# Attention units taken in pairs, and a tile's rows turned behind a pair's turns

## The chip, the cores and the metric

One Trainium2 chip (trn2), one core. The metric is the device time of the whole kernel in microseconds: the median of three runs, beside one profiled execution with its trace.

## The reference

Three stages follow on each other, all in float32 at the interface.

- Attention: batch 4, 8 heads, 576 positions, head size 64. Scores are q·kᵀ/8; a score lower than its row's maximum less tau is dropped; softmax over what is left; product with v.
- A mixture of experts over the 2304 tokens of width 512: noisy logits (x·w_gate plus log(1 + exp(x·w_noise)) times noise), the two highest of 8 experts, softmax of the two; each expert is relu(x·w1)·w2 with 1024 hidden channels.
- A dense layer pair with 2048 hidden channels and a leaky relu with a slope per channel, giving the output of 2304 × 512.

## The kernel before, in words

The whole program is written out by hand, one instruction after another, and each engine works through its own instructions in the order in which they are emitted. The change lies in the attention stage, up to about 300 us.

**Units.** The 80 entries of `units` (lines 323 to 329) are the attention's steps. A whole unit is one batch, one block of 128 queries and one pair of heads; four units (the four pairs of heads) make up one tile of 128 tokens, 18 tiles in all. The last 64 queries of a batch make tail units ("t", one score block for both heads): units 16 to 23 and 56 to 63.

**The pieces of a unit**, each a small function (lines 333 to 438):

- `s_mm` (L347): the scores on TensorE, 12 matmuls (6 for a tail unit) from q and k split into high and low parts, into one PSUM tile `ps_s` for each head. There are two of these tiles.
- `d1` (L358): VectorE scales and negates the scores into `m_tmp` and takes their minimum. `thresh` (L363, ScalarE) makes the threshold from it.
- `a1` (L369, ScalarE): the exponentials into `m_hh`, once for each head.
- `d2` (L382, VectorE): drops what lies under the threshold and sums the rest.
- `t_mm` (L399 to L403): TensorE turns the 128 × 1152 exponentials, nine 128 × 128 matmuls with an identity, in three parts of four, four and one, each into one PSUM tile `ps_t`; `a2` (L411 to L415) is ScalarE's copy of each part out of PSUM. There are three `ps_t` tiles for everything that is turned or summed in passing.
- `pv` (L432 to L437): 20 matmuls with V into the tile `ps_v`, of which there is one. After a tile's fourth unit `group_evac` (L460, ScalarE) copies it out.

**A tile's own steps** (`x_stages`, from line 465): `rows` turns the four blocks of the tile (L481) into a `ps_t` tile, and VectorE multiplies them with the inverse sums (L471, L472, L483), after which SP stores them (L485); `logits` (L491, ScalarE copy L494), `flip` (L498, one turn into a `ps_t` tile) and `sum_` (L502, L505 on VectorE, which frees that tile). `gating` (from line 515) ranks the tokens of a group of tiles and sends their rows to the experts by indirect DMA on GpSimd (L600); its `rank` also holds a `ps_t` tile until `place` has read it.

**The order.** A table `at` holds work by (iteration, part): splits of q and k for later batches (ScalarE L289 and L291, GpSimd L299), loads, weights (L170, L173), and the tile's own steps. The loop at lines 720 to 769 emits in iteration i: the turns of unit i - 2, `d1` and `a1` of unit i, `d2` of unit i - 1, the scores of unit i + 1, the table's part 0, the product with V of unit i - 3, the table's part 1. So for TensorE each unit is turns, scores, V, and a tile's rows come between V and the next turns:

```python
                        for j, p, f in todo:
                            put((j, p), f)
            ...
            for f, a in at.pop((i, 1), []):
                f(*a)
```

Of the kernel before, what the change touches and what calls it, by code (L numbers as in the profile page):

```python
# [14 lines left out]
HP = H // 2  # L15
# [18 lines left out]
def emit(tc, qt, kt, v, tau, wg, wn, noise, w1, w2, w_in, w_out, alpha, out):  # L34
# [8 lines left out]
    with (  # L43
# [289 lines left out]
        def s_mm(i):  # L333
            b, c, hp = units[i]
            qh, ql, kh, kl, zh, zl = sets[b * HP + hp]
            u = st[i]
            for h in range(nh(i)):
                u["ps", h] = psum_s()
            q0 = 0 if c == "t" else c * 128 + (64 if b % 2 else 0)
            for x in range(2):  # L340
                for k, (q, z, kk) in enumerate(((qh, zh, kh), (qh, zh, kl), (ql, zl, kh))):
                    for h in range(nh(i)):

                        r = slice(0, 128) if c == "t" else slice(h * 64, h * 64 + 64)
                        lhs = z if c == "t" else q[r, q0:q0 + 128]
                        o = (64 - 64 * h) + x * 288
                        pe.matmul(u["ps", h][:, x, :288], lhs, kk[r, o:o + 288], start=(k == 0), stop=(k == 2))  # L347

        def nh(i):
            return 1 if units[i][1] == "t" else 2  # L350

        def d1(i, h):
            u = st[i]
            if h == 0:
                u["sp"] = sp_ring()
                u["sm"] = sm_ring()
            ps = u.pop(("ps", h))
            dve.tensor_scalar(u["sp"][:, h].rearrange("p (a b) -> p a b", a=2), ps[:, :, :288],  # L358
                              -0.125, None, op0=OP.mult, op1=OP.min, accum_out=u["sm"][:, h:h + 1])
# [30 lines left out]
        def t_mm(i, part):  # L390
            u = st[i]
            em = u["em"]
            emf = em.rearrange("p h s -> p (h s)")
            ps = psum_t()
            u["pt", part] = ps
            if part < 2:
                o = part * 640
                for j in range(4):
                    pe.transpose(ps[:, j * 128:j * 128 + 128], emf[:, o + j * 128:o + j * 128 + 128], ident)  # L399
            elif nh(i) == 2:  # L400
                pe.transpose(ps[:, :128], emf[:, 512:640], ident)
            else:
                pe.transpose(ps[:64, :128], emf[:, 512:576], ident)  # L403
# [241 lines left out]
        def put(i, f, *a):  # L645
            at.setdefault(i if isinstance(i, tuple) else (i, 1), []).append((f, a))
# [69 lines left out]
                f(*a)  # L716

        END = NU + DT + 1
        s_mm(0)
        for i in range(END):  # L720
            it, iv = i - DT, i - DT - 1
            tiles, outs = 0 <= it < NU, 0 <= iv < NU
            if tiles:
                t_mm(it, 0)
                a2(it, 0)
            if i < NU:
                for h in range(nh(i)):
                    d1(i, h)
                for h in range(nh(i)):
                    a1(i, h)  # L730
            if 0 < i <= NU:
                for h in range(nh(i - 1)):
                    d2(i - 1, h)
            if tiles and nh(it) == 2:
                t_mm(it, 1)
                a2(it, 1)
            if tiles:
                t_mm(it, 2)
                a2(it, 2)
            if i < NU:  # L740
                thresh(i)
            if i + 1 < NU:
                s_mm(i + 1)
            for f, a in at.pop((i, 0), []):
                f(*a)
            if i == END - 1:
                do_fill()
            if outs:
                pv(iv)
                if units[iv][2] == HP - 1 or iv < SOLO:  # L750
                    T = group_evac(iv)
                    if T is not None:
                        todo = [(i + (1, 3, 5, 7, 2)[T] + d if T < 5 else i + 1 + d, p, f) for d, p, f in x_stages(T)]
                        if T == NT - 1:
                            last_rows.append(todo[0][2])
                            todo = [(i + 1, 0, todo[1][2]), (i + 1, 0, todo[4][2]), (i + 2, 0, todo[2][2]), (i + 2, 0, todo[3][2])]
                        else:
                            todo = todo[:4]
                        if T == NT - 2:
                            todo = [(i + d, p, f[2]) for (d, p), f in zip(((1, 1), (1, 1), (2, 1), (2, 1)), todo)]  # L760
                        for t0, t1 in GROUPS:
                            if T == t1 - 1:
                                todo += [(i + {3: 8, NT - 1: 3, NT: 2}.get(t1, 4) + d, p, f) for d, p, f in gating(t0, t1)]
                        for j, p, f in todo:
                            put((j, p), f)
            if i >= NU:
                do_fill()
            for f, a in at.pop((i, 1), []):
                f(*a)
        for t in range(BLOCK0 // 128, CAP // 128):  # L770
            put((END + 2, 2), x_load, 0, t)
        rest = {(END, 0): 1, (END + 1, 1): 2}
# [370 lines left out]
```

## Time and profile before

| | |
|---|---|
| median of three runs | 1194.61 us (1193.58 to 1195.39) |
| the profiled execution | 1195.54 us |
| its span, first to last instruction | 1193.8 us |
| TensorE (PE) busy | 1158.9 us, 97% |
| VectorE (DVE) busy | 584.0 us, 49% |
| ScalarE (ACT) busy | 529.4 us, 44% |
| GpSimd (POOL) busy | 512.5 us, 43% |

PE rows are matmuls, whose ends are modelled, so a start is a better mark than an end; a row of the timeline merges instructions of one line that follow on each other ("x8"), with the time from the first start to the last end. An idle time in brackets stands before the row, with what ended it. L411 is line 411 of the kernel. The attention stage is the first quarter of the span, and there the other engines are busy for most of the time too.

### The profile page before, as it was taken

The page shows a single profiled execution, that of the slowest core. Times are in us where ns is not written, and L with a number is a line of the kernel's source. Part 1 is how long each engine was busy: PE and PEld are TensorE (multiplying, and loading weights), DVE is VectorE, ACT ScalarE, POOL GpSimd, SP SyncE. Part 2 cuts the span into 40 slices and gives each one's busy share as a digit, 9 for nine tenths or more (in the row PEclk, how much of TensorE's full clock was granted, in tenths as well). Part 3 has the DMA queues.
Part 4 walks back from the last instruction along what each step waited for, and adds up shares of the span by engine and source line. Part 5 has one row for each costly group of instructions (what it writes and reads, how often), then busy time and mean ns, then how long its engine had stood idle before and what let it go on. Part 6 is the DMA issues. An engine that isn't in the chain of part 4 may idle for free. (4 is left out here: it accounts for less than half of the span.)

```text
span 1193.8 us, 20318 instructions
## 1 busy us (share of the span) xinstructions
PE 1158.9 (97%) x7942; PEld 996.7 (83%) x7942; DVE 584.0 (49%) x1285; ACT 529.4 (44%) x1039; POOL 512.5 (43%) x555
## 2 busy tenths in 40 slices
PE   7998999999899999999999999999999999999997
PEld 6887777877788989888989898988888888888886
DVE  7978888799533344334435332434333333333221
ACT  7977778788434444444444443533111211211111
POOL 7736435543515444444544454545332332332221
PEclk9999999999999999999999999999999999999999
DMA  7423222132335555456554556542100200200001
GB/s 222 127 85 131 79 93 72 69 146 90 142 132 178 202 177 175 168 176 208 191 192 161 176 169 204 175 145 67 53 19 18 71 18 18 71 19 18 36 1 37
DMA packets 60597, 135.19 MB, mean 113 GB/s; under 512 B 9680, under 2 KB 10320, under 8 KB 60496
## 3 DMA queue, kind: packets, MB, share of 16 engines
q1 hardware_dynamic: 54448, 114.61, 28.4%
q0 software_dynamic: 5760, 18.88, 4.7%
q8 instruction: 64, 1.05, 0.3%
q10 hardware_dynamic: 288, 0.34, 0.1%
q14 instruction: 37, 0.30, 0.1%
HBM read 93.96 MB, written 39.85 MB: 112 GB/s over the span
## 5 line engine op out<-in xcount | busy, mean ns | idle before, releaser
L197 PE MATMUL ps_t<-m_v,m_pair 128*128 128x384 f32 (+2 forms) x1216 | 220.9, 318 | 2.0 <-DVE m_gate L208 2.0
L173 POOL TENSOR_TENSOR m_pair<-m_v,m_pair 128x1024 fp32r<-128x1024 f32 x57 | 139.5, 2448 | 140.9 <-ACT m_pair L170 140.7
L197 PEld LDWEIGHTS ps_t<-m_v,m_pair 128*128 128x128 f32 x1216 | 187.0, 190 | 10.6 <-DVE m_gate L208 2.5
L215 PE MATMUL ps_s<-m_pair,m_hh 128*128 128x512 f32 x528 | 175.6, 396 | 0.0
L968 DVE TENSOR_SCALAR m_tmp<-ps_t,alpha_t 128x512 f32<-128x512 f32 (+1 forms) x80 | 55.7, 696 | 218.1 <-PE ps_t L197 218.1
L208 DVE SCALAR_TENSOR_TENSOR m_gate<-ps_t,m_hh 128x384 fp32r<-128x384 f32 (+1 forms) x120 | 58.3, 493 | 153.1 <-ACT m_hh L207 153.0
L197 PE MATMUL ps_t<-m_v,m_early 128*128 128x256 f32 (+2 forms) x672 | 127.4, 320 | 1.3 <-ACT m_v L189 0.8
L382 DVE SCALAR_TENSOR_TENSOR m_hh<-m_tmp,sm,m_hh 128x576 f32<-128x576 f32 x144 | 127.2, 915 | 1.7 <-ACT sm L363 1.3
L215 PEld LDWEIGHTS ps_s<-m_pair,m_hh 128*128 128x128 f32 x528 | 99.2, 188 | 20.3
L973 POOL TENSOR_TENSOR m_v<-m_tmp,m_v 128x512 fp32r<-128x512 f32 x39 | 50.3, 1290 | 149.1 <-ACT m_v L972 149.1
L358 DVE TENSOR_SCALAR_CACHE_REDUCE m_tmp<-ps_s 128x576 f32<-128x576 f32 x144 | 103.5, 752 | 16.3 <-PE ps_s L347 15.8
L197 PEld LDWEIGHTS ps_t<-m_v,m_early 128*128 128x128 f32 x672 | 105.9, 189 | 6.5 <-ACT m_v L189 1.1
L369 ACT ACTIVATE m_hh<-m_tmp,sm 128x576 f32<-128x576 f32 x144 | 105.7, 782 | 12.6 <-DVE m_tmp L358 12.5
L347 PE MATMUL ps_s<-m_pair 64*128 64x288 f32 (+1 forms) x864 | 95.7, 320 | 12.9 <-DVE m_tmp L358 8.3
L215 PE MATMUL ps_s<-m_pair,m_gate 128*128 128x512 f32 x264 | 103.4, 392 | 0.0
L972 ACT CAST m_v<-m_tmp 128x512 fp32r<-128x512 f32 x39 | 24.2, 621 | 177.1 <-DVE m_tmp L969 177.1
L347 PEld LDWEIGHTS ps_s<-m_pair 64*128 64x128 f32 (+1 forms) x864 | 72.9, 192 | 28.0 <-DVE m_tmp L358 13.9
L992 PE MATMUL ps_s<-m_pair,m_v 128*128 128x512 f32 x396 | 95.9, 391 | 0.0
L973 POOL TENSOR_TENSOR m_gate<-m_tmp,m_gate 128x512 fp32r<-128x512 f32 (+1 forms) x41 | 45.1, 1101 | 114.2 <-ACT m_gate L972 109.9
L207 ACT ACTIVATE m_hh<-ps_t 128x384 fp32r<-128x384 f32 (+1 forms) x120 | 52.0, 440 | 93.7 <-PE ps_t L197 92.5
L992 PE MATMUL ps_s<-m_pair,m_gate 128*128 128x512 f32 x360 | 89.2, 393 | 0.0
L992 PEld LDWEIGHTS ps_s<-m_pair,m_v 128*128 128x128 f32 x396 | 73.9, 188 | 15.3
(226 smaller groups left out, 1979.8 us busy)
## 6 DMA issues: line engine op xcount, KB each, us to landing
m_v<-in_w_dram SPq DMA_DIRECT2D x64, 512.0 KB, 3.5
yg<-m_tmp SPq DMA_DIRECT2D x40, 256.0 KB, 2.3
m_tmp<-in_w_in_dram SPq DMA_DIRECT2D x16, 512.0 KB, 4.8
m_tmp<-in_w_out_dram SPq DMA_DIRECT2D x16, 512.0 KB, 4.6
m_v<-xg SPq DMA_DIRECT2D x20, 256.0 KB, 4.4
m_rows<-xg SPq DMA_DIRECT2D x20, 256.0 KB, 4.0
m_early<-in_kt_dram SPq DMA_DIRECT2D x15, 320.0 KB, 3.3
yg<-m_gate SPq DMA_DIRECT2D x18, 256.0 KB, 2.0
```

Of the source, the lines that this page charges most:

```text
L173: eng.tensor_tensor(WL[n], wraw.pop(n), f32(WH[n]), op=OP.subtract)
L197: pe.matmul(ps[:, :n], w[wc[d]][:, col:col + 128], x[xx][:, d, :n], start=(k == 0), stop=(k == 11))
L207: act.activation(h, ps, AF.Relu)
L208: dve.scalar_tensor_tensor(hs[1][:, f * n:f * n + n], ps, 0.0, f32(h), op0=OP.max, op1=OP.subtract)
L215: pe.matmul(ps, a[:, o:o + 128], ww[w][:, c:c + 512], start=(f == 0 and k == 0), stop=(f == nf - 1 and k == 2))
L347: pe.matmul(u["ps", h][:, x, :288], lhs, kk[r, o:o + 288], start=(k == 0), stop=(k == 2))
L358: dve.tensor_scalar(u["sp"][:, h].rearrange("p (a b) -> p a b", a=2), ps[:, :, :288], -0.125, None, op0=OP.mult, op1=OP.min, accum_out=u[" ...
L369: act.activation(u["em"][:, h], u["sp"][:, h], AF.Exp, bias=u["sm"][:, h:h + 1], scale=-1.0)
L382: dve.scalar_tensor_tensor(u["em"][:, h], u["sp"][:, h], sm[:, 2 + h:3 + h], u["em"][:, h], op0=OP.is_le, op1=OP.mult, accum_out=acc)
L968: dve.tensor_scalar(g, ps, 0.0, alpha_t[:, f:f + 1], op0=OP.min, op1=OP.mult)
L973: pool.tensor_tensor(h[:, n:2 * n], g, f32(h[:, :n]), op=OP.subtract)
L992: pe.matmul(ps, h[x][:, t * 128:t * 128 + 128], ww[w][:, c:c + 512], start=(f == 0 and k == 0), stop=(f == 15 and k == 2))
```

## The change

Units 20 to 75 are no longer taken one by one but in pairs (`two(k)` for even k from 20 to 74). For a pair TensorE gets: the turns of units k - 4 and k - 3, a tile's rows if they are due (the table's new part -1), the scores of unit k, the product with V of units k - 4 and k - 3, logits, the scores of unit k + 1, the flip. On ScalarE the six copies of the turns follow on each other; `group_evac` comes between the two exponentials of unit k. `rows` moves from part 1 of an iteration to part -1 of the next. Before unit 20 and from 76 on, `one(i)` keeps the old order (the three turns of a unit are now emitted together, which leaves each engine's order as it was, and rows come behind the turns). At 76 a short block leads from one order to the other.

```diff
--- before.py
+++ after.py
@@ -716,57 +716,124 @@
                 f(*a)
 
         END = NU + DT + 1
-        s_mm(0)
-        for i in range(END):
+
+
+        PAIR0, PAIR1 = 20, 76
+        done = set()
+
+        def once(f, n, *a):
+            if 0 <= n < NU and (f, n) not in done:
+                done.add((f, n))
+                f(n, *a)
+
+        def parts(n):
+            return (0, 1, 2) if nh(n) == 2 else (0, 2)
+
+        def turn_all(n):
+            for part in parts(n):
+                t_mm(n, part)
+                a2(n, part)
+
+        def d1_all(n):
+            for h in range(nh(n)):
+                d1(n, h)
+
+        def a1_all(n):
+            for h in range(nh(n)):
+                a1(n, h)
+
+        def d2_all(n):
+            for h in range(nh(n)):
+                d2(n, h)
+
+        def events(i, p):
+            for f, a in at.pop((i, p), []):
+                f(*a)
+
+        def weigh(iv, i):
+            pv(iv)
+            if units[iv][2] == HP - 1 or iv < SOLO:
+                T = group_evac(iv)
+                if T is not None:
+                    todo = [(i + (1, 3, 5, 7, 2)[T] + d if T < 5 else i + 1 + d, p, f) for d, p, f in x_stages(T)]
+                    if T == NT - 1:
+                        last_rows.append(todo[0][2])
+                        todo = [(i + 1, 0, todo[1][2]), (i + 1, 0, todo[4][2]), (i + 2, 0, todo[2][2]), (i + 2, 0, todo[3][2])]
+                    else:
+                        todo = [(todo[0][0] + 1, -1, todo[0][2])] + todo[1:4]
+                    if T == NT - 2:
+                        todo = [(i + d, p, f[2]) for (d, p), f in zip(((1, 1), (1, 1), (2, 1), (2, 1)), todo)]
+                    for t0, t1 in GROUPS:
+                        if T == t1 - 1:
+                            todo += [(i + {3: 8, NT - 1: 3, NT: 2}.get(t1, 4) + d, p, f) for d, p, f in gating(t0, t1)]
+                    for j, p, f in todo:
+                        put((j, p), f)
+
+        def two(k):
+            for n in (k - 4, k - 3):
+                once(turn_all, n)
+            once(d1_all, k - 1)
+            once(thresh, k - 1)
+            once(a1_all, k - 1)
+            once(d2_all, k - 2)
+            events(k, -1)
+            events(k + 1, -1)
+            events(k, 0)
+            once(s_mm, k)
+            once(d1_all, k)
+            a1(k, 0)
+            for n in (k - 4, k - 3):
+                once(weigh, n, k)
+            for h in range(1, nh(k)):
+                a1(k, h)
+            thresh(k)
+            done.update(((a1_all, k), (thresh, k)))
+            once(d2_all, k - 1)
+            events(k, 1)
+            once(s_mm, k + 1)
+            events(k + 1, 0)
+            events(k + 1, 1)
+
+        def one(i):
             it, iv = i - DT, i - DT - 1
-            tiles, outs = 0 <= it < NU, 0 <= iv < NU
-            if tiles:
-                t_mm(it, 0)
+            if 0 <= it < NU:
+                for part in parts(it):
+                    t_mm(it, part)
                 a2(it, 0)
-            if i < NU:
-                for h in range(nh(i)):
-                    d1(i, h)
-                for h in range(nh(i)):
-                    a1(i, h)
-            if 0 < i <= NU:
-                for h in range(nh(i - 1)):
-                    d2(i - 1, h)
-            if tiles and nh(it) == 2:
-                t_mm(it, 1)
-                a2(it, 1)
-            if tiles:
-                t_mm(it, 2)
-                a2(it, 2)
-            if i < NU:
-                thresh(i)
-            if i + 1 < NU:
-                s_mm(i + 1)
-            for f, a in at.pop((i, 0), []):
-                f(*a)
+                done.add((turn_all, it))
+            once(d1_all, i)
+            events(i, -1)
+            once(a1_all, i)
+            once(d2_all, i - 1)
+            if 0 <= it < NU:
+                for part in parts(it)[1:]:
+                    a2(it, part)
+            once(thresh, i)
+            once(s_mm, i + 1)
+            events(i, 0)
             if i == END - 1:
                 do_fill()
-            if outs:
-                pv(iv)
-                if units[iv][2] == HP - 1 or iv < SOLO:
-                    T = group_evac(iv)
-                    if T is not None:
-                        todo = [(i + (1, 3, 5, 7, 2)[T] + d if T < 5 else i + 1 + d, p, f) for d, p, f in x_stages(T)]
-                        if T == NT - 1:
-                            last_rows.append(todo[0][2])
-                            todo = [(i + 1, 0, todo[1][2]), (i + 1, 0, todo[4][2]), (i + 2, 0, todo[2][2]), (i + 2, 0, todo[3][2])]
-                        else:
-                            todo = todo[:4]
-                        if T == NT - 2:
-                            todo = [(i + d, p, f[2]) for (d, p), f in zip(((1, 1), (1, 1), (2, 1), (2, 1)), todo)]
-                        for t0, t1 in GROUPS:
-                            if T == t1 - 1:
-                                todo += [(i + {3: 8, NT - 1: 3, NT: 2}.get(t1, 4) + d, p, f) for d, p, f in gating(t0, t1)]
-                        for j, p, f in todo:
-                            put((j, p), f)
+            once(weigh, iv, i)
             if i >= NU:
                 do_fill()
-            for f, a in at.pop((i, 1), []):
-                f(*a)
+            events(i, 1)
+
+        once(s_mm, 0)
+        for i in range(END):
+            if i == PAIR1:
+                for n in (i - 4, i - 3):
+                    once(turn_all, n)
+                once(d1_all, i - 1)
+                once(thresh, i - 1)
+                once(a1_all, i - 1)
+                once(d2_all, i - 2)
+                once(s_mm, i)
+                once(weigh, i - 4, i)
+            if PAIR0 <= i < PAIR1:
+                if (i - PAIR0) % 2 == 0:
+                    two(i)
+            else:
+                one(i)
         for t in range(BLOCK0 // 128, CAP // 128):
             put((END + 2, 2), x_load, 0, t)
         rest = {(END, 0): 1, (END + 1, 1): 2}
```

## Rows read from the trace of the kernel before

**Rows 1.** Windows: us; busy us (count) of PE, PEld, DVE, ACT, POOL; clock, DMA

```profile
70.47:286.21 215.74, 202.84 (x2411) 166.07 (x2410) 184.10 (x529) 168.22 (x374) 100.90 (x188) 0.99 0.27 94
...
121.10:124.51 3.41, 3.41 (x29) 3.13 (x31) 3.25 (x9) 1.52 (x5) 2.46 (x3) 0.50 0.80 276
```

**Rows 2.** Timeline of PE, 161 to 171 us: start, us, instruction, [idle before <-releaser]

```profile
161.20 0.33 PE L498 MATMUL ps_t<-ident,m_rows 128*128 128x128 f32 x1
161.36 1.04 PE L399 MATMUL ps_t<-ident,m_hh 128*128 128x128 f32 x8
162.69 0.33 PE L401 MATMUL ps_t<-ident,m_hh 128*128 128x128 f32 x1 [0.29 <-ACT m_tmp L411]
162.95 1.05 PE L347 MATMUL ps_s<-m_pair 64*128 64x288 f32 x12
163.94 1.09 PE L435 MATMUL ps_v<-m_last,m_v 128*64 128x128 f32 x16
...
165.18 1.09 PE L399 MATMUL ps_t<-ident,m_hh 128*128 128x128 f32 x8
...
166.31 1.05 PE L347 MATMUL ps_s<-m_pair 64*128 64x288 f32 x12
...
168.54 0.66 PE L481 MATMUL ps_t<-ident,m_last 128*128 128x128 f32 x4
...
170.65 0.40 PE L347 MATMUL ps_s<-m_pair 64*128 64x288 f32 x1 [0.34 <-DVE m_tmp L358]
171.33 1.05 PE L347 MATMUL ps_s<-m_pair 64*128 64x288 f32 x11 [0.28 <-DVE m_tmp L358]
```

**Rows 3.** Timeline of DVE, 164 to 170 us

```profile
164.04 0.76 DVE L358 TENSOR_SCALAR_CACHE_REDUCE m_tmp<-ps_s 128x576 f32<-128x576 f32 x1 [0.36 <-PE ps_s L347]
...
165.40 0.82 DVE L382 SCALAR_TENSOR_TENSOR m_hh<-m_tmp,sm,m_hh 128x576 f32<-128x576 f32 x1
...
169.23 0.69 DVE L483 TENSOR_TENSOR m_gate<-ps_t,es 128x512 f32<-128x512 f32 x1 [1.95 <-PE ps_t L481]
```

**Rows 4.** Timeline of ACT, 162 to 169 us

```profile
162.06 0.59 ACT L411 COPY m_tmp<-ps_t 128x512 f32<-128x512 f32 x1 [0.70 <-PE ps_t L399]
...
166.41 1.44 ACT L369 ACTIVATE m_hh<-m_tmp,sm 128x576 f32<-128x576 f32 x2
167.75 0.57 ACT L411 COPY m_last<-ps_t 128x512 f32<-128x512 f32 x1
168.22 0.27 ACT L413 COPY m_last<-ps_t 128x128 f32<-128x128 f32 x1
...
168.57 0.67 ACT L289 CAST m_pair<-m_early 128x576 fp32r<-128x576 f32 x1
```

**Rows 5.** Timeline of PE, 75 to 79 us, tail units

```profile
75.59 0.42 PE L491 MATMUL ps_t<-m_hh,m_rows 128*32 128x128 f32 x8
75.95 0.66 PE L399 MATMUL ps_t<-ident,m_hh 128*128 128x128 f32 x4
76.44 0.27 PE L403 MATMUL ps_t<-ident,m_hh 128*64 128x128 f32 x1
76.47 1.04 PE L347 MATMUL ps_s<-m_pair 128*128 128x288 f32 x6
...
78.33 0.33 PE L498 MATMUL ps_t<-ident,m_rows 128*128 128x128 f32 x1
```

**Rows 6.** Timeline of PE, 119 to 125 us

```profile
119.68 0.33 PE L401 MATMUL ps_t<-ident,m_hh 128*128 128x128 f32 x1 [1.55 <-DVE m_gate L483]
...
121.03 1.77 PE L347 MATMUL ps_s<-m_pair 64*128 64x288 f32 x11 [0.28 <-DVE m_tmp L358]
122.73 1.94 PE L435 MATMUL ps_v<-m_last,m_v 128*64 128x128 f32 x16
```

**Rows 7.** Timeline of PE, 268 to 273 us

```profile
268.97 0.66 PE L481 MATMUL ps_t<-ident,m_tmp 128*128 128x128 f32 x4
...
272.12 0.39 PE L347 MATMUL ps_s<-m_pair 64*128 64x288 f32 x1 [0.34 <-DVE m_tmp L358]
```

## Prediction

> **What bounds the kernel now.** I read the profile page first (TensorE is busy nearly all through the span), then the table of windows, then the timeline of the attention stage engine by engine. The change touches only the stretch between the turns of unit 18 at 70.47 us and the row turns at 286.21 us: 215.74 us, the "stretch" from here on. There TensorE is busy 202.84 us, VectorE 184.10 and ScalarE 168.22 [rows 1], so three engines are close together and small waits count.
>
> TensorE works through one unit as three blocks. In an undisturbed unit the scores start at 162.95, the products with V at 163.94, the next turns at 165.18, the next scores at 166.31 [rows 2]: 0.99 + 1.24 + 1.13 = 3.36 us. Inside a block of turns the step from matmul to matmul is (1.09 - 0.27)/7 = 0.117 us (eight in 1.09, one lasts 0.27) [rows 2, 5]; the ninth starts 0.93 after the first, so the change to the scores takes 0.20. By the same working the other two changes of block take 0.22 (scores to V) and 0.20 (V to turns), against steps of about 0.07 and 0.05 inside those blocks. Two units in the old order have six changes.
>
> Two things disturb the old order. Where a tile's rows are turned (168.54), VectorE has stood idle 1.95 us for them [rows 3]; its minimum of the unit's scores comes after it in the queue, and the next scores start at 170.65, that is 2.11 after the row turns where 0.49 + 1.13 = 1.62 would do; their second matmul comes at 171.33 instead of one step of 0.07 on, some 0.61 more [rows 2]. Where a flip stands ahead of the turns, it holds one of the three PSUM tiles until VectorE has summed it, and the third tile of turns waits until ScalarE has copied the first: 162.69 instead of 162.29, so 0.40, and with it the scores [rows 2]. A tile (four units) so costs 13.44 + rows, logits and flip 1.01 + waits 1.5, nearly 16 us.
>
> **The change part by part.** First the gain. In the new order two units need turns, scores, V twice, scores: four changes instead of six. With changes of 0.20 and 0.22 (V to scores and scores to turns occur nowhere before: the bounds are the step inside a block, 0.05, and 0.24; I take 0.20 and 0.22, the nearest changes of block), and no wait: turns 2.18, scores 0.98, V 1.04 + 0.05 + 1.25 = 2.34, scores 0.98, together 6.48 against 6.72.
>
> Second, the wait that comes in. Six tiles of turns now follow on each other, and three PSUM tiles take them. ScalarE starts the first copy 0.70 to 0.75 after the first turn [rows 4], the copy lasts 0.58, TensorE goes on about 0.06 after its end (162.06 + 0.59, then 162.69) [rows 2, 4]. Counting from the first turn: the copies follow at 0.47 [rows 4]; tile 4 can start at 0.75 + 0.58 + 0.06 = 1.39 instead of 1.05, tile 5 when copy 2 ends, at 1.88, tile 6 at 2.32, scores at 2.52. That is 0.34 more than 2.18: a pair without rows or flip costs 6.82, and the gain of the fewer changes is gone.
>
> Third, a flip is now turned at the end of one pair and summed only behind the next pair's turns, so those run on two PSUM tiles: tile 3 at 1.39, tile 4 at 1.88, tile 5 at 2.36, and tile 6 waits for the copy of tile 4 (ready 2.61, ends 3.19), so 3.25 and scores at 3.51. A held pair costs 7.81, 0.99 for the hold where the old order paid 0.40. The ranks of a group of tiles hold a PSUM tile in the same way over three pairs.
>
> Fourth, the rows. Turned behind the six tiles, they wait for copy 4 (2.13 + 0.58 + 0.06 = 2.77), last 0.37 and give way to the scores at 3.34. VectorE by then has done the two minima (1.36 for two) and the two masked sums (0.82 each) [rows 3], so it no longer waits for rows with a minimum behind it: rows cost 0.82 instead of 0.49 + 0.49 + 0.61. With logits 0.36 [rows 5] and flip 0.16 [rows 2] such a pair costs 3.34 + 0.98 + 2.34 + 0.36 + 0.98 + 0.16 = 8.16; held, the rows wait for the copy of tile 5 (3.73) and it costs 9.12. The rows' store stands in SP's queue until the multiply is done; behind it are loads for units several pairs ahead, so I price that at nothing: what hides it is that lead, and without it the rounding on ScalarE, and by it the turns, would wait as long as the store is late. The scatters on GpSimd keep their pairs; the rows that kept a turn waiting at 119.68 [rows 6] come more than half a pair later against them, which ends that wait.
>
> Fifth, ScalarE. The copy that empties the V tile now waits for two units' products and stands ahead of the second half of the exponentials. In a held pair: scores 3.51, V from 4.49, last product done at 6.99; the copy, exponential (1.34 for two) and threshold are through at 8.33 [rows 4], the pair ends at 7.81, and the next first copy is due at 8.56. It is in time by 0.2. Where a split of q or k follows (0.6, six held pairs) the six copies start 0.38 late; where a weight is rounded in its place (two pairs) 0.73. VectorE is through before each new minimum: in the held pair it starts at 4.60, then 1.36 + 1.64 = 7.60 us, and its next is due at 8.9.
>
> The sum. Of the 28 pairs 18 are of whole units: 6 with rows at 8.16 = 48.96; 3 held with rows at 9.12 = 27.36; 9 held at 7.81, one with a flip of its own, = 70.45. The ten with tail units in them go by the same steps (two tail units' turns end 1.39 us in, or 1.88 held; tail scores follow turns of the same form at once, at 76.47 after 76.44; from there to the flip at 78.33 are 1.86, 0.98 for the scores as in a whole unit and 0.88 for V, of which two cost 1.65, one change being saved [rows 5]): 2.9, 7.2, 5.4, 6.2, 8.0, 7.6, 6.1, 5.6, 5.8, 5.3 = 60.1. The crossing back to single units 4.74; ranks and closing 0.7; late copies 6 x 0.38 + 2 x 0.73 = 3.8. Together 216.1 us against 215.74. Behind the stretch, the last rows turned in single units lose their wait, about -1.0. So the change comes to -0.6 us. The profiled execution took 1195.54 us (span 1193.8), 0.9 above the median of the three runs, 1194.61; from that median I get 1194.0. The old stretch contains single losses that I let go with it: the wait at 119.68 (1.55) and what followed [rows 6].
>
> **The rivals.** About 0.2%, 2.4 us, is what a measurement here can tell from no change.
> (a) *Faster, the hold is short.* If VectorE sums the flip before tile 3 needs its place, the 16 holds cost nothing: 16 x 0.96 = 15 us, 1179. Against it stand the waits in front of the third tile that the old order shows [rows 2]; for it, that VectorE has a microsecond to spare in a pair. Half of that gives 1186.
> (b) *Faster, the two unseen changes of block cost no more than a step.* 28 x (0.15 + 0.13) = 7.8 us, 1186. Against it: each change seen takes about 0.2.
> (c) *Slower, ScalarE is late behind every V copy.* 13 pairs hold such a copy, and the margin in each is 0.2 us; beyond it what ScalarE is late is paid one to one. 0.38 more in each, as one more split would make it, is 4.9 us, and 0.73 more, as another weight would, 9.5: 1199 to 1203. It decides from 0.2 us of extra ScalarE work or of later products. For it speaks that ScalarE is busy for 168 of the stretch's 216 us [rows 1], against it that its copies in the turns have no other work between them.
> (d) *Slower, the clock falls.* In the old trace the granted clock drops to 0.50 (1.2 GHz) from 121.10 to 124.51 [rows 1], behind turns whose last one had waited 1.55; the eleven scores then take 1.77 and the sixteen products 1.94 instead of 1.09 [rows 2, 6], in all 1.6 us. The row turns and turns from 268.97 to 272.12 did not bring it down [rows 7]. The new turns run 3.34 with rows, 3.67 with a flip before them, 4.3 in held rows: all longer than the 3.15 us that did not bring it down. If idle time is what counts there is no fall, as the new gaps are 0.3 us and shorter. If turns themselves do not count, up to 16 stretches are paid, 16 x 1.6 = 25 us: 1220; two falls already pass 2.4 us. The Trainium skill says in TensorE: Matmul & The Clock Gate, Part 4: PE-mode transpose, that transposes do not count as busy in the way other matmuls do; by that rule the outcome would be this one. The trace agrees with it at 121.10 and does not decide it, as that stretch was also idle.
> (e) *The order of the engines stays as it was*: not likely, as each engine takes its instructions in the order they are written. It would give 1194.6.
>
> **How the numbers follow.** My forecast has 0.40 (its own range, with each pair good to 0.1 us and 1 us of losses that I don't see, 1190 to 1198: 0.23 same, 0.11 faster, 0.06 slower). (a) 0.15, faster. (b) 0.15, of it 0.14 faster. (c) 0.18, of it 0.17 slower. (d) 0.10, slower. (e) 0.02. Faster 0.40, same 0.27, slower 0.33. The range goes from 1184 (half of (a), all of (b)) to 1204 (all of (c), a few falls of (d)).
>
> **What would show it.** In the profile after: ScalarE as the releaser of waits in front of the fourth, fifth and sixth tile of turns, about 0.3 us a pair, 1.3 in held ones; rows starting 2.8 us into a pair, with VectorE idle before its multiply but no wait of the scores for the minimum; 6.8 to 9.1 us from pair to pair. No waits before the turns would prove the sum wrong on the fast side; ScalarE busy without a gap ahead of the first copy, or a granted clock of 0.50 behind long turns, on the slow side.

## The result, and the profile after

The changed kernel takes 1210.59 us (median of four runs, 1209.76 to 1211.91) against 1195.00 for the kernel before on the same chip: ratio 1.0138, 95% interval 1.0123 to 1.0154. It is slower by 15.6 us, and the forecast of 1194.0 with its range to 1204 was wrong. The profiled execution took 1211.91 us, its span 1210.2 (before: 1193.8); the difference of the spans, 16.4 us, is what the traces have to explain.

First the windows of the changed kernel (us; busy us and count of PE, PEld, DVE, ACT, POOL; granted clock; DMA share, GB/s). The first five are stages, cut where the scores of units 20, 28, 56, 68, 76 and 79 start; four single stretches follow.

```profile
71.44:102.69 31.25, 27.74 (x327) 21.66 (x324) 21.86 (x69) 20.31 (x51) 11.17 (x33) 0.95 0.18 64
102.69:221.25 118.56, 106.11 (x1255) 86.38 (x1255) 104.58 (x292) 92.64 (x200) 55.91 (x100) 1.00 0.28 96
221.25:259.52 38.27, 35.62 (x448) 29.84 (x446) 28.91 (x89) 28.26 (x69) 17.16 (x44) 1.00 0.20 77
259.52:296.50 36.98, 30.33 (x352) 24.94 (x351) 32.37 (x78) 27.73 (x59) 14.87 (x12) 0.97 0.31 108
296.50:313.46 16.96, 14.07 (x137) 11.51 (x136) 13.07 (x40) 9.90 (x21) 3.50 (x6) 0.86 0.22 79
...
294.44:297.85 3.41, 3.41 (x19) 3.08 (x21) 0.00 (x0) 2.60 (x7) 3.18 (x5) 0.50 0.01 4
308.09:311.50 3.41, 3.41 (x31) 3.13 (x31) 3.35 (x11) 1.42 (x4) 0.00 (x0) 0.50 0.28 105
183.65:186.81 3.16, 2.46 (x20) 1.91 (x18) 3.06 (x7) 3.02 (x9) 2.23 (x5) 1.00 0.00 0
175.87:179.34 3.47, 2.72 (x20) 1.94 (x19) 3.44 (x10) 2.17 (x5) 1.66 (x2) 1.00 0.50 199
```

TensorE's work is the same in both kernels, so a stage is longer by waits (36.98 - 30.33 = 6.65 us without a matmul from 259.52 to 296.50) or by a lower clock. Cut at the same units, the stages of all kernels of this study are (us, from the starts of the scores in each trace):

| kernel | units 20 to 28 | 28 to 56 | 56 to 68 | 68 to 76 | 76 to 79 | after that |
|---|---|---|---|---|---|---|
| before | 25.63 | 118.26 | 34.69 | 34.38 | 12.99 | 896.93 |
| changed | 31.25 | 118.56 | 38.27 | 36.98 | 16.96 | 896.73 |
| e1 rows only | 24.69 | 117.48 | 35.04 | 31.60 | 17.73 | 897.80 |
| e2 pairs 28 to 56 | 24.68 | 120.00 | 34.96 | 31.59 | 17.74 | 898.55 |
| e3 flip after | 27.26 | 116.81 | 38.38 | 32.86 | 16.35 | 894.64 |
| e4 end 72 | 29.76 | 118.46 | 38.25 | 32.33 | 16.85 | 895.40 |
| e5 rows, ranks | 24.69 | 112.18 | 35.53 | 31.54 | 15.33 | 899.18 |
| e6 and one-hot | 24.69 | 111.87 | 35.55 | 31.55 | 12.88 | 898.30 |
| e7 pairs mended | 26.75 | 109.46 | 37.16 | 30.85 | 12.88 | 899.35 |
| e8 old rows | 28.28 | 116.77 | 37.75 | 34.21 | 11.53 | 895.40 |
| e9 mended, old rows | 26.30 | 112.36 | 36.61 | 30.11 | 13.26 | 897.53 |
| e10 ranks alone | 29.75 | 114.15 | 37.58 | 36.08 | 16.35 | 898.27 |
| e11 one-hot alone | 29.75 | 118.27 | 38.28 | 36.06 | 12.32 | 894.90 |
| e12 one row late | 26.29 | 108.82 | 36.86 | 30.11 | 13.25 | 898.24 |

Each row is one profiled execution, and falls of the clock, about 1.5 us each, come and go between executions; a stage can differ by that much for no other reason.

In the long middle, 28 whole units, the change costs 0.3 us; it would be more if the kernel before did not lose some 3.2 us there at one place that the change avoids, the wait of 1.55 us and the slow clock behind it [rows 6]. Most of the loss lies at the edges: 5.6, 3.6, 2.6 and 4.0 us.

Now the rows that answer to [rows 2] and [rows 6]: TensorE's timeline of the changed kernel (start, us, instruction, idle before and what ended it). From 175.87 one regular cycle of two pairs; then single places.

```profile
150.34 0.17 PE L565 MATMUL ps_t<-m_gate 128*128 128x24 bf16 x1 [0.78 <-DVE m_gate L560]
...
175.87 1.04 PE L399 MATMUL ps_t<-ident,m_hh 128*128 128x128 f32 x8
177.21 0.33 PE L401 MATMUL ps_t<-ident,m_hh 128*128 128x128 f32 x1 [0.29 <-ACT m_tmp L411]
177.69 1.09 PE L399 MATMUL ps_t<-ident,m_hh 128*128 128x128 f32 x8 [0.16 <-ACT m_tmp L411]
179.08 0.33 PE L401 MATMUL ps_t<-ident,m_hh 128*128 128x128 f32 x1 [0.29 <-ACT m_last L411]
179.34 1.05 PE L347 MATMUL ps_s<-m_pair 64*128 64x288 f32 x12
180.32 1.09 PE L435 MATMUL ps_v<-m_tmp,m_v 128*64 128x128 f32 x16
...
183.65 1.09 PE L399 MATMUL ps_t<-ident,m_hh 128*128 128x128 f32 x8
184.58 0.27 PE L401 MATMUL ps_t<-ident,m_hh 128*128 128x128 f32 x1
185.43 1.14 PE L399 MATMUL ps_t<-ident,m_hh 128*128 128x128 f32 x8 [0.57 <-ACT m_tmp L411]
186.41 0.27 PE L401 MATMUL ps_t<-ident,m_hh 128*128 128x128 f32 x1
186.82 0.66 PE L481 MATMUL ps_t<-ident,m_hh 128*128 128x128 f32 x4
187.40 1.06 PE L347 MATMUL ps_s<-m_pair 64*128 64x288 f32 x12
...
192.06 0.33 PE L498 MATMUL ps_t<-ident,m_rows 128*128 128x128 f32 x1
192.23 1.04 PE L399 MATMUL ps_t<-ident,m_hh 128*128 128x128 f32 x8
...
265.43 0.33 PE L498 MATMUL ps_t<-ident,m_rows 128*128 128x128 f32 x1 [1.03 <-ACT m_rows L494]
...
294.39 1.96 PE L399 MATMUL ps_t<-ident,m_hh 128*128 128x128 f32 x8 [2.18 <-ACT m_tmp L411]
...
307.24 0.40 PE L347 MATMUL ps_s<-m_pair 64*128 64x288 f32 x1 [2.13 <-DVE m_tmp L358]
```

The pair from 175.87 has a flip ahead of it: scores come 3.47 us after the first turn (forecast 3.51), the pair takes 183.65 - 175.87 = 7.78 (7.81). The pair from 183.65 has rows: they start 3.17 in, the scores 3.75 in, and it takes 192.23 - 183.65 = 8.58 (8.16 and 0.38 for the late copies). The cycle is 16.36 us, as the forecast's steps give (16.35). The same cycle took 16.07 before, from 166.31 [rows 2] to the scores at 182.38:

```profile
182.38 1.05 PE L347 MATMUL ps_s<-m_pair 64*128 64x288 f32 x12
```

The single places have other causes, each on another engine. ScalarE's timeline of the changed kernel, answering to [rows 4]:

```profile
184.23 0.66 ACT L289 CAST m_pair<-m_early 128x576 fp32r<-128x576 f32 x1
184.79 1.07 ACT L411 COPY m_tmp<-ps_t 128x512 f32<-128x512 f32 x2
...
264.18 1.03 ACT L170 CAST m_early<-m_v 128x1024 fp32r<-128x1024 f32 x1
265.12 0.26 ACT L494 COPY m_rows<-ps_t 128x128 f32<-128x128 f32 x1
...
291.49 1.03 ACT L170 CAST m_pair<-m_v 128x1024 fp32r<-128x1024 f32 x1
292.42 0.22 ACT L528 ACTIVATE m_gate<-m_rows 128x24 f32<-128x24 f32 x1
293.39 0.22 ACT L540 ACTIVATE m_gate<-m_gate 128x24 f32<-128x24 f32 x1 [0.75 <-POOL m_gate L533]
293.64 0.22 ACT L541 ACTIVATE m_gate<-m_gate 128x24 f32<-128x24 f32 x1
293.77 1.06 ACT L411 COPY m_tmp<-ps_t 128x512 f32<-128x512 f32 x2
```

At 184.79 the first copy is late behind a split, as forecast: turns started at 183.65, the copy 1.14 later instead of 0.73. At 265.12 the logits' copy stands behind a weight's rounding, and the flip, which needs that copy, holds up TensorE by 1.03 us. At 293.77, where pairs end, the first copy of the turns of 291.01 stands behind a weight, three steps of the gating and a wait for GpSimd.

VectorE and GpSimd of the changed kernel at 304 us:

```profile
304.25 2.04 DVE L558 TENSOR_TENSOR m_gate<-m_gate,ix 128x48 f32<-128x48 f32 x1
...
306.42 0.75 DVE L358 TENSOR_SCALAR_CACHE_REDUCE m_tmp<-ps_s 128x576 f32<-128x576 f32 x1
```

```profile
303.86 2.36 POOL L173 TENSOR_TENSOR m_pair<-m_v,m_pair 128x1024 fp32r<-128x1024 f32 x1 [5.99 <-ACT m_pair L170]
```

The one-hot of a gating group takes 2.04 us beside GpSimd's work on a weight; the minimum of the scores stands behind it, the scores at 307.24 wait, and the clock is at 0.50 from 308.09. In the kernel before the same instruction took 0.21 us, at 291.08, before GpSimd began on its weight at 291.59:

```profile
291.08 0.21 DVE L558 TENSOR_TENSOR m_gate<-m_gate,ix 128x48 f32<-128x48 f32 x1
...
291.59 2.38 POOL L173 TENSOR_TENSOR m_pair<-m_v,m_pair 128x1024 fp32r<-128x1024 f32 x1 [1.83 <-ACT m_pair L170]
```

### The profile page after: what moved, and what is told of

The parts are those of the page before. It is cut to its first block, busy times and chain, and to the rows that moved or that the text cites. A ratio compares the mean times of both kernels' runs of the same rounds, so it can differ in the third digit from the quotient of the medians.

```text
span 1210.2 us, 20292 instructions
## 1 busy us (share of the span) xinstructions
PE 1160.2 (96%) x7942; PEld 997.8 (82%) x7942; DVE 591.3 (49%) x1285; ACT 531.4 (44%) x1039; POOL 509.0 (42%) x555
## 5 line engine op out<-in xcount | busy, mean ns | idle before, releaser
L347 PE MATMUL ps_s<-m_pair 64*128 64x288 f32 (+1 forms) x864 | 92.0, 321 | 9.5 <-DVE m_tmp L358 4.8
L399 PE MATMUL ps_t<-ident,m_hh 128*128 128x128 f32 x576 | 81.5, 283 | 10.6 <-ACT m_tmp L411 9.8
```

## The experiments

The kernel before ran beside each group on the same chip: median 1194.74 us beside e1 to e4, 1193.69 beside e5 to e8, 1194.13 beside e9 to e11, 1194.35 beside e12. The groups ran on different chips, so between two groups the ratios compare better than the times.

**e1: rows behind the turns, no pairs.**

```diff
-        PAIR0, PAIR1 = 20, 76
+        PAIR0, PAIR1 = 0, 0
-            if i == PAIR1:
+            if i == PAIR1 and i:
```

> No pairs at all: every unit alone as before, and only the rows of a tile turned behind a unit's turns. Theory A (three PSUM tiles for six tiles of turns eat what the pairs save, single losses at the pairs' two ends do the rest, and the rows' new place is a gain by itself): rows cost 1.39 + 0.37 + 0.20 - 1.13 = 0.83 us instead of 0.49 + 0.49 + 0.61, about 0.76 less for each of some 15 tiles, so about 1184 us, faster than before. Theory B (the rows' new place is what costs, since they now stand between the turns and the scores): slower than before, 1200 or more. Theory C (any shift of this stage brings VectorE and ScalarE out of step): no better than before, 1195 to 1200.

Measured: 1195.27 us, ratio 1.0002 (0.999 to 1.0014), 11 us off the 1184 of the first theory. The regular cycle did shrink, to 15.27 us (scores at 163.46 and 178.73). What was gained there, and by the end of the wait of [rows 6], went at two places with ranks and one at the end. TensorE's timeline of e1, with the first of them:

```profile
147.06 0.19 PE L570 MATMUL ps_t<-m_gate 128*128 128x16 bf16 x2
147.12 1.07 PE L399 MATMUL ps_t<-ident,m_hh 128*128 128x128 f32 x8
148.48 0.33 PE L401 MATMUL ps_t<-ident,m_hh 128*128 128x128 f32 x1 [0.29 <-ACT m_tmp L411]
150.29 0.75 PE L481 MATMUL ps_t<-ident,m_gate 128*128 128x128 f32 x4 [1.48 <-ACT m_tmp L411]
...
163.46 1.05 PE L347 MATMUL ps_s<-m_pair 64*128 64x288 f32 x12
...
178.73 1.05 PE L347 MATMUL ps_s<-m_pair 64*128 64x288 f32 x12
```

The ranks' tile stays taken until VectorE reads it, and VectorE's queue has the rows' multiplication ahead of that; so the rows need the second tile of turns to be copied, and ScalarE does that after two exponentials (copy at 149.67). The rows come 3.18 us after the first turn instead of 1.39, and the granted clock is 0.50 from 150.73. The same happens at 200.40, and a one-hot of 2.02 us stands ahead of the scores at 290.71.

**e2: pairs for units 28 to 55 alone** (`PAIR0, PAIR1 = 28, 56`).

> Pairs only from unit 28 to 55, 14 of the 28, all of whole units; rows behind the turns throughout. Theory A: these 14 pairs cost what the units cost before (118.6 against 118.3 us in the two traces), the single units outside gain by the rows' new place, one or two single losses at the new crossings: 1190 us, 1187 to 1196. Theory B (each pair costs the same, 15.6 us over 28): half of the loss stays, about 1203 us.

Measured: 1198.09 us, ratio 1.003 (1.0016 to 1.0044), between the two. The stages say why: the stage with the pairs is 1.7 us longer (120.00 against 118.26), with a wait of 1.45 us for a minimum near its beginning (102.92); units 68 to 76 in the old order with the rows moved gain 2.8; and the last stage, where the one-hot takes 2.03 us, loses 4.7.

**e3: the flip behind the first scores of a pair, and summed at once**, in pairs alone.

```diff
+                        j = todo[3][0]
+                        if j % 2 == 0 and PAIR0 <= j < PAIR1:
+                            todo[2:] = [(j, 0, todo[2][2]), (j, 2, todo[3][2])]
...
             once(d1_all, k)
+            events(k, 2)
```

> Pairs as in the changed kernel, but the flip of a tile is turned behind the next pair's turns and summed right after the first minima of that pair, so it no longer holds one of the three PSUM tiles during the turns. Theory A: 11 held pairs lose about 0.97 us each, so 10 to 11 us less than the changed kernel, about 1200 us, and in the turns of those pairs the third tile no longer waits for the copy of the first. Theory D (the turns wait for ScalarE, which is busy with other work, and not for a free place): no more than 2 us less, 1208 to 1211.

Measured: 1200.46 us, ratio 1.0059 (1.0039 to 1.0079): 10.1 us less than the changed kernel (9.4 by the ratios). The number is that of the first theory, but only half of it by the theory's way. The pair that was held takes 7.34 instead of 7.77 us, 0.43 less and not 0.97: behind six tiles the flip waits for a place as rows do, and the scores come 3.03 us after the first turn (121.58 to 124.61) instead of 3.47. For 11 such pairs that is 4.7 us. The stage of units 68 to 76, where flips waited 1.03 and 0.96 us for the logits' copy, loses 4.1 us, and that of units 20 to 28 4.0, some 1.5 of it the fall at 79.40 that e3's trace does not have.

**e4: pairs to unit 72** (`PAIR0, PAIR1 = 20, 72`).

> Pairs from unit 20 to 71 only, so the crossing back to single units comes four units earlier, away from the third-last group's gating on ScalarE. Theory A: the turns of 5.1 us at the crossing, the wait of 2.4 us behind it and the two falls of the clock there go, some 6 us less than the changed kernel: 1204 us, 1202 to 1206. Theory B (each pair costs the same): two pairs fewer of 28, 1.1 us less, 1209.5 us.

Measured: 1206.38 us, ratio 1.0103 (1.0086 to 1.012), 4.2 us less, where the first theory had 6. The stage of units 68 to 76 goes from 36.98 to 32.33 us; the one-hot behind it stays (16.85).

**e5: e1 with the ranks beside their reader.**

```diff
-  plan = ... + [(5, 1, rank), (6, 0, place)]
+  plan = ... + [(6, 0, rank), (6, 0, place)]
...
-  plan = ... + [(4, 1, rank), (5, 0, place)]
+  plan = ... + [(5, 0, rank), (5, 0, place)]
```

> The kernel of e1 (single units, rows behind the turns) with the ranks' matmuls moved from the end of the iteration ahead of the rows to the place of their reader, behind the next scores. Theory A: in e1 the ranks hold a PSUM tile over the turns and the rows, since their reader stands behind the rows' multiplication on VectorE; turns to rows took 3.18 and 3.46 us there instead of 1.39, and the clock fell behind both. Without the hold the two places lose 3.3 and 3.6 us, with them two of e1's four clock falls: 1195.3 - 6.9 = 1188.4 (1187 to 1190). Rival B: the waits are ScalarE's own work ahead of the copies (exponentials, splits), and the ranks only happen to stand there: 1195, falls unchanged.

Measured: 1192.01 us, ratio 0.9985 (0.9973 to 0.9998), 3.3 us less than e1, about 2 by the ratios. In the stage of units 28 to 56 it is 5.3 us less, and the falls at 150.73 and 201.93 are gone: the tile that the ranks held is shown as the cause. The two traces differ by 5.6 us, but that of e1 is 2.1 us above the median of its runs; against the 6.9 us expected the gain stays small.

**e6: e5 with the two best of tiles 12 to 14 one unit later** (the same line of the program serves tiles 0 to 2, so theirs move too).

```diff
-  plan = [(d // 2, 1, f) for d, f in enumerate(first)] + ...
+  plan = [((0, 0, 1, 1, 3)[d], 1, f) for d, f in enumerate(first)] + ...
```

> e5 and the two best of the group of tiles 12 to 14 (with their one-hot rows) one unit later. Theory A: in e1 the one-hot instruction took 2.02 us on VectorE at 287.74 because GpSimd was working on the low half of a weight from 287.35 for 2.35 us; the scores waited 2.11 us and the clock fell. A unit later the instruction takes its 0.2 us; turns, scores, products and turns get back 2.2 + 1.4 + 1.1 + 0.5 = 5.2 us: 1188.4 - 5.2 = 1183 (1182 to 1186), and no fall before 300 us is left. Rival B: the long one-hot is by its own inputs, not by GpSimd: it stays at 2 us, one unit later, and the time at 1188.

Measured: 1189.76 us, ratio 0.9973 (0.9963 to 0.9983). The one-hot took 0.21 us, the last stage 12.88 instead of 15.33. That last stage gives 2.5 us of the expected 5.2: in e5 the scores had waited 2.12 us behind the one-hot, but the clock had not fallen there as it had in e1, so less was to be had. A fall at 299.69 us stays, behind the units' end.

**e7: the changed kernel with all four mends** (e3, e4, ranks, one-hot).

> The changed kernel with four mends together: flips turned behind the first scores and summed at once (e3), pairs to 72 only (e4), the ranks beside their reader, the two best of tiles 12 to 14 one unit later. Theory A: what the changed kernel loses are these single places, and they add up: 1210.6 - 10.1 (e3) - 4.2 (e4) - 2 x 2.2 (ranks: the wait of 1.44 and a held pair's 0.8) - 3.5 (one-hot and the fall behind it) = 1188.4 (1186 to 1192), faster than before. Rival B: the pairs themselves are longer than single units (ScalarE's copies in the six tiles), and mends only move the waits: not under 1194.

Measured: 1189.19 us, ratio 0.9968 (0.9958 to 0.9978), where the first theory had 1188.4. So the four losses add up, to more than the change had cost. Three of them are single places; the hold of the flips recurs in every tile. Units 28 to 56 take 109.46 us, against 111.87 in e6 with single units, though the regular cycle of a tile is still longer than in e1 (15.76 us, turns at 118.52 and 134.28, against 15.27): the mended pairs win in the other tiles.

**e8: the changed kernel with rows where they were, ahead of a pair's turns.**

```diff
-                            todo = [(todo[0][0] + 1, -1, todo[0][2])] + todo[1:4]
+                            todo = todo[:4]
```

> The changed kernel with the rows of a tile turned where they were, at the end of an iteration ahead of the next turns. Theory A (the fourth part of the prediction): rows ahead of a pair's turns cost 0.49 and hold a PSUM tile over them, 0.99, against 0.82 behind them: 0.66 more in each of 9 to 13 pairs, 1216.5 to 1219. Rival B: in pairs the rows behind six tiles cost more than they save, as they hold up the scores: 1205 or less.

Measured: 1199.16 us, ratio 1.0056 (1.0039 to 1.0073): 11.4 us *less* (9.8 by the ratios), the opposite of what I expected. TensorE's timeline of e8 around such a place, and VectorE's:

```profile
171.84 1.04 PE L399 MATMUL ps_t<-ident,m_hh 128*128 128x128 f32 x8
...
179.62 0.66 PE L481 MATMUL ps_t<-ident,m_hh 128*128 128x128 f32 x4
180.12 1.04 PE L399 MATMUL ps_t<-ident,m_hh 128*128 128x128 f32 x8
181.06 0.33 PE L401 MATMUL ps_t<-ident,m_hh 128*128 128x128 f32 x1
181.45 1.15 PE L399 MATMUL ps_t<-ident,m_hh 128*128 128x128 f32 x8
...
182.64 1.06 PE L347 MATMUL ps_s<-m_pair 64*128 64x288 f32 x12
...
187.46 1.04 PE L399 MATMUL ps_t<-ident,m_hh 128*128 128x128 f32 x8
```

```profile
180.32 0.69 DVE L483 TENSOR_TENSOR m_gate<-ps_t,es 128x512 f32<-128x512 f32 x1 [0.68 <-PE ps_t L481]
```

VectorE was waiting for the rows and is done with them at 181.01, before the third tile needs their place at 181.06. They hold nothing up here: the scores come 2.52 us after the first turn, as in a pair without rows, and the rows cost 0.49. They also give ScalarE 0.49 us more before the first copy, so a split no longer makes it late. Behind six tiles rows cost 3.75 - 2.52 = 1.23. The cycle is 15.62 us (171.84 to 187.46). Side by side, the regular cycle of a tile in the four kernels:

| | rows ahead of the turns | rows behind them |
|---|---|---|
| single units | 16.07 (before) | 15.27 (e1) |
| pairs | 15.62 (e8) | 16.36 (changed) |

Each half of the change alone shortens the regular cycle; together they lengthen it. Neither half alone makes the whole kernel faster (ratios 1.0056 and 1.0002), because of the single places. The larger part of e8's gain is not the cycle either: units 28 to 56 gain 1.8 us, and the last stage 5.4 (11.53 against 16.96), where the one-hot took 0.21 us at 293.56, ahead of GpSimd's weight at 294.74, although no edit had aimed at it.

**e9: e7 with the old rows** (the edits of e7 and e8).

> The kernel of e7 (pairs to 72, flips behind the first scores, ranks beside their reader, the late one-hot) with the rows of a tile turned where they were, ahead of a pair's turns. Theory A: the two edits of the change get in each other's way: behind six tiles the rows are a seventh and wait for ScalarE's fourth copy, ahead of them VectorE takes them before the third tile needs their place. By the blocks of e7 and e8 a tile (two pairs) then takes 7.83 + 7.18 = 15.0 us against 15.76 in e7 and 15.3 in e1; over some ten tiles 7 us: 1182 (1180 to 1185), the fastest of all. Rival B: rows ahead hold a PSUM tile over the turns as a flip does (the prediction's fourth part), 0.66 more a tile: 1196.

Measured: 1189.45 us, ratio 0.9959 (0.9942 to 0.9975). The cycle was 15.02 us as expected (168.88 to 183.90), but the time was 7 us above the first theory. One place gave 3 us back. VectorE's and TensorE's timelines of e9:

```profile
114.53 0.69 DVE L483 TENSOR_TENSOR m_gate<-ps_t,es 128x512 f32<-128x512 f32 x1 [2.64 <-DMA xg<-m_gate,posi]
```

```profile
115.28 0.33 PE L401 MATMUL ps_t<-ident,m_hh 128*128 128x128 f32 x1 [2.66 <-DVE m_gate L483]
```

The multiplication writes into rows that a group's scatters are still reading. It is the wait of [rows 6] at 119.68, which the moved rows do avoid: that part of the change is worth having, at this one place.

Two more tiles lost as well. Where a group's two best stand ahead of the rows' multiplication in VectorE's queue, the third tile of turns waits for it, 1.01 us at 147.49 and 1.02 at 193.69, and these tiles take 16.15 us against 15.35 and 15.66 in e7. So rows ahead of the turns hold nothing up only where VectorE is free for them.

**e10: the changed kernel with the ranks beside their reader, and no more** (the edit of e5).

> The changed kernel with the ranks beside their reader and nothing else. Theory A: the ranks cost the changed kernel their wait for VectorE's one-hot (0.78 and 0.77 us at 145 and 195 us) and the held pair behind (9.14 instead of 8.5): 2 x 1.4 = 2.9 us less, 1207.7 (1206 to 1209). Rival B: turns or copies wait as long without them: 1210 or more.

Measured: 1205.80 us, ratio 1.0098 (1.0068 to 1.0128), 4.8 us less, where the first theory had 2.9 (its two waits stand at 150.34 and 200.74). The stage of units 28 to 56 is 4.4 us shorter; five pairs shrink by 0.6 to 1.0 us each (30, 38, 40, 50 and 52).

**e11: the changed kernel with the late one-hot, and no more** (the edit of e6).

> The changed kernel with the two best of tiles 12 to 14 one unit later and nothing else. Theory A: the scores at 307 us waited 2.13 us for a minimum that stood behind a one-hot of 2.04 us on VectorE, beside GpSimd's work on a weight, and the clock fell behind that wait (1.5 us): 3.6 us less, 1207.0 (1205.5 to 1208.5), no fall at 308. Rival B: the late units wait for something else just behind (ScalarE's copies): 1209.5 to 1211.

Measured: 1205.31 us, ratio 1.0094 (1.0065 to 1.0123), 5.3 us less. VectorE's timeline of e11:

```profile
304.92 0.21 DVE L558 TENSOR_TENSOR m_gate<-m_gate,ix 128x48 f32<-128x48 f32 x1
```

GpSimd's weight ran from 300.51 for 2.39 us here, and no longer beside it. The last stage is 4.6 us shorter, and no fall is left before the end of the attention. The edit did not cause all of that: the crossing's wait of 2.18 us, ahead of the one-hot, is still there (292.58), and in this execution the clock did not fall behind it.

**e12: e9 with that one tile's rows behind the turns.**

```diff
                             todo = todo[:4]
+                            if i == 30:
+                                todo[0] = (todo[0][0] + 1, -1, todo[0][2])
```

> The kernel of e9 with one tile's rows (those at 111.09 us) behind the pair's turns, as in the change; all other rows ahead of them. Theory A: in e9 this one multiplication waited 2.64 us on VectorE for scatters that still read the rows of an earlier tile, the second tile of turns waited 2.66 us for its PSUM place and the clock fell behind it: the pair took 11.12 us. Turned behind the six tiles, the rows meet the scatters' end, and the pair takes about 8.1 as in e7 at 110.47: 3.0 us less, 1186.4 (1185 to 1188), no fall before 1180 us. Rival B: the wait goes to the next rows or to the ranks, and the time stays at 1189.

Measured: 1186.31 us, ratio 0.9937 (0.9923 to 0.995), as the first theory had it: the pair at 110.44 takes 8.06 us instead of 11.12. This is the fastest kernel of the study, 24 us under the changed one. A fall at 295.20 us, behind the units' end, remains. The stage of units 56 to 68, which holds the tail units, still takes 36.86 us against 34.69 in the old order, so pairs might better be left out there; that was not tried.

## Why the prediction was wrong

**What held.** The five steps for regular pairs held to a tenth of a microsecond: held turns 3.47 (3.51), held pair 7.78 (7.81), rows with late copies 8.58 (8.54), held rows 9.14 (9.12), two pairs 16.36 (16.35). (From the end of a copy to the next tile the quoted rows give 0.04 us, not 0.06; a held pair has that step three times.) The unseen changes of block cost the 0.20 and 0.22 assumed, so rival (b) fell. The holds were paid in full, so (a) fell. (e) fell with the order of the rows above.

**What failed** are the terms for places that occur once or twice. By span the change cost 16.4 us against -0.6; the 17.0 us between them come apart like this:

- *The stretch's beginning*, 2.3 us. The turns at 70.47 are unit 17's, not unit 18's; the sum of the pairs stands against 72.79 to 286.21, 213.4 us, not 215.74. By the prediction's own steps the change should have come to +1.7 us. The pairs then began 0.5 us later than before.
- *The ten mixed pairs*, forecast 60.1, measured 63.3: 3.2 us. Flips waited 0.38 us at 76.54 and 0.71 at 98.36 for the logits' copy, and the granted clock was 0.50 from 79.40, about 1.5 us. That fall is in no other kernel with this order up to there (e4, e10, e11: 29.75 us for the stage instead of 31.25), so it is an accident of this execution rather than of the change.
- *The 18 whole pairs with "ranks and closing 0.7; late copies 3.8"*, forecast 151.3, measured 154.4: 3.2 us. Mis-sized were the ranks: they wait for VectorE's one-hot at 150.34 and again in pair 50, and pairs 28, 30, 38 and 50 were 3.3 us over their prices where I had 0.7 (pair 28, 10.35 for 9.12, by a queue of two best, rows and sum ahead of a minimum). The flips at 265.43 and, two pairs on, 0.96 us late, put pairs 68 and 72 at 9.73 and 9.89 for 8.89 (8.16 and a late weight's 0.73): I had looked for late ScalarE work in front of the six copies alone, and the weight stood in front of the logits' copy. Against that, only three of the six splits made the copies late, 1.0 us less than priced. That the holds of pairs 40 and 52 (9.14 for 9.12) were in the sum is why e10, which also takes those away, gives back more than was mis-sized.
- *The crossing back to single units*, forecast 4.74, measured 8.33: 3.6 us. I had counted its matmuls and not asked what ScalarE's queue holds there (a weight, three steps of gating, a wait of 0.75 for GpSimd). That queue explains some 2.1 us. The other 1.5 are the fall at 294.44: in e10 and e11 the same wait of 2.18 us brought no fall, and the crossing took 6.79 and 6.80. TensorE's timeline of e10 there:

```profile
288.19 1.14 PE L399 MATMUL ps_t<-ident,m_hh 128*128 128x128 f32 x8 [2.18 <-ACT m_tmp L411]
```

- *Behind the stretch*, forecast -1.0, measured +3.3 (16.4 of the span, less 0.5 and less 63.3 + 154.4 + 8.3 - 213.4 = 12.6): 4.3 us. That the one-hot would fall beside GpSimd's weight was not among the steps; moving it gave 5.3 us back (e11), by the medians. In this execution the fall at 308.09 is part of it.

Added up: 2.3 + 0.5 + 3.2 + 3.2 + 3.6 + 4.3 = 17.1.

**The rivals on the slow side.** Rival (c), ScalarE late behind every V copy, has the right engine and the wrong place: the copies were late by 0.4 where a split stood, as forecast, and the larger waits arose in front of the logits' copy and at the crossing. Rival (d), the clock falling behind long turns, gave 1220 by another mechanism. The long turns of whole pairs did not bring the clock down once: the stretches from 183.65 to 186.81 and, held, from 175.87 to 179.34 were granted 1.00. There were three falls, not sixteen, about 4.5 us; those at 294.44 and 308.09 came behind waits of 2.18 and 2.13 us. The rule of the Trainium skill (TensorE: Matmul & The Clock Gate, Part 4: PE-mode transpose) that transposes do not count as busy in the way other matmuls do would have had a fall in each such stretch; the trace does not agree with it here.

**What the prediction did not ask** is whether the rows belong behind a pair's turns at all. The price of the rows there was right (0.82 and 0.38 against 1.23 measured); that they cost 0.49 ahead of the turns, and in a regular tile hold nothing, came out in e8 alone.

## What to carry to other kernels

A forecast for a reordered loop needs two lists: the regular iteration, and every place where something else stands in an engine's queue (a group's ranks, a weight's rounding, the end of the new order), each walked with the queues of all engines. Here the first was good to 0.1 us an iteration and the second was 15 us off. Two reorderings that each shorten the regular cycle can lengthen it together when both lean on the same engine's copies; try them one at a time, and read the stages besides the time, as a gain can come from a place that nobody aimed at (e3, e8). A tile of PSUM should be taken next to the instruction that reads it out, not an iteration earlier: that alone was worth about 2 us in single units (e5) and 5 in pairs (e10).

## What the hardware showed

- A VectorE instruction on 128 × 48 elements took 2.04 us (2.02 in e1) while GpSimd worked on 128 × 1024 elements for 2.36 us, and 0.21 us wherever GpSimd was not at that (before, e6, e11). Beside a shorter GpSimd instruction of 0.80 us it took 0.79 (100.25, changed kernel). That GpSimd slows it is shown by moving it; how it does so is not.
- The falls of the granted clock to 0.50 that the traces show by the turns stand behind waits of TensorE: 1.48 us in e1, 2.66 in e9, 2.18 and 2.13 in the changed kernel, 1.55 before [rows 6], and once, at 79.40, three waits of 0.38, 0.62 and 0.62 in a row. Long turns with short waits brought none: 0.29, 0.16 and 0.29 us (held, 175.87) or one of 0.57 (185.43).
- A wait that brings a fall in one execution need not bring one in another. The crossing's 2.18 us had a fall behind it in the changed kernel and none in e10 and e11, and 2.12 us behind the one-hot had none in e5. Where a fall came it cost about 1.5 us beside the wait: the crossing took 8.33 us with it and 6.79 without, the pair from 76.71 8.69 with it and 7.20 in e4. What decides between the two is not shown.
